# Issuing filler matmuls two at a time behind every second value step, in a fused attention and state-space kernel

## The chip, the cores and the metric

The kernel runs on one core of one Trainium2 chip, as one launch. The metric is the time of the launch on the device in microseconds, as the median of several runs; one more execution is taken with the hardware profiler, and its trace is what this document reads. Engines are called as the profile calls them: PE (TensorE's matmuls), PEld (its weight loads), DVE (VectorE), ACT (ScalarE), POOL (GpSimd) and SP (SyncE, which only issues DMAs here).

## The reference

Two independent results of 2048 x 640 are put side by side. The first is an attention in which each position sees only 8 earlier positions, 2 apart; the second is a long convolution (a state-space layer) done by Fourier transforms:

```python
# A: 32 heads of 20, window W = 8, dilation 2
q, k, v = split(x @ wqkv)                       # x: 2048 x 640
logits[h, s, w] = q[h, s] . k[h, s - 2 w] * 20 ** -0.5   # -1e9 where s - 2 w < 0
attn = softmax(logits, over w)
o[h, s] = sum_w attn[h, s, w] * v[h, s - 2 w]
a = o.reshape(2048, 640) @ wo
# B: K is a kernel of length L = 2048 for each of 640 channels, from 192 modes
K = Re sum_n Cc[d, n] * exp(dt[d] * A[d, n] * l) * dt[d] * Bc[d, n]
y = irfft(rfft(u padded to 2 L) * rfft(K padded to 2 L))[:L] + u * Dskip
out = concatenate([a, y], axis=-1)              # bf16, 2048 x 1280
```

## The kernel before

The kernel first makes the convolution's kernel K for five chunks of channels, transforms K and u, multiplies, and runs the first half of the inverse transform, whose result goes to DRAM (`Zd`). The attention's projections and logits are woven into the end of this. All that the change concerns is the last stage, from about 355 us on: the loop at the end of `body` (lines 847 to 888), where three kinds of work meet.

*Value steps.* The attention's sum over w is done by `Attention.av_step` (L608). The loop runs over 6 groups of (positions, head rows) and in each over w = 0 to 7, which makes 48 steps; the text numbers them s = 8·group + w. A step is one VectorE product of v with the weights (L618, into one of 6 ring buffers `ring`, so that product s + 6 can only be written when TensorE has read product s) and 16 matmuls of 32x32 tiles with the identity, which add the product up in two PSUM tiles `ps_o`. At w = 7 ScalarE copies the two tiles to `o` (L629); the tiles come from a pool of three, so the second half of the next group's first step waits for the first of these copies.

*Parts of the last inverse step.* `Inverse.part` (L676) makes 2 or 3 of the 64 rows l0 of y: 8 or 12 matmuls from a quarter of Z, which is loaded back from `Zd` by `Inverse.load` (L666) on SP's queue and, for the first and last quarter, also on POOL's; then one ScalarE copy to `ysb` (L687), and after each third part four writes of y on SP's queue (L690). There are 24 parts, p0 to p23, the last quarter of Z being read by p18 to p23. The ring of `ysb` has four places of three parts each.

*Output pieces.* `Attention.out_piece` (L631) makes a tile of 128 positions x 320 columns of `o @ wo`: 5 matmuls, one copy to `ob` (ScalarE, L645; VectorE, L643, for every second of the last eight), and after each second piece one write on POOL's queue (on SP's for the last four). Eight pieces come free with `out_proj` after each of the groups 1, 2, 4 and 5; they wait in the list `rest`, the parts in the list `parts`.

`fill(some, n)` (L839) issues the next n entries of a list. The parts and the pieces take their PSUM tiles from the same pool of two banks (`Attention.one`), in which the sums of the second softmax, `ps_s` (L572, matmuls at steps 6, 8, 11 and 14), hold one bank until `reciprocal` (L577) has read it, in VectorE's order after step 19.

`att.in_order()` (L833) makes TensorE's matmuls and ScalarE's copies of this stage keep the order in which the program issues them; VectorE's products keep it too. TensorE, ScalarE, VectorE and each DMA queue work their instructions off in order, so a wait of one instruction holds up all that stands behind it on its engine.

In group 1 one part follows each step from w = 2 on; in group 2 one piece each of the first three steps, five pieces the fourth, and one part each of the others; in groups 3 and 4 pieces and parts take turns, one behind each step; in group 5 one piece follows each step. What is left, the eight pieces of the last group, follows the loop.

Of the kernel before, what the change touches and what calls it, by code (L numbers as in the profile page):

```python
# [695 lines left out]
def body(tc, ctx, pools, prm, B_u, B_Dskip, Sd, Zd, UDd, A_x, A_wqkv, A_wo, out_a, out_b):  # L696
# [14 lines left out]
    with tc.tile_pool(name="prep_l", bufs=1) as pl, tc.tile_pool(name="prep_d", bufs=1) as pd, tc.tile_pool(name="prep_g", bufs=1) as pg, tc.tile_pool(name="prep_h", bufs=1) as ph, tc.tile_pool(name="psum_p", bufs=2, space=bass.MemoryType.PSUM) as psp:  # L711
        pools.update(prep_l=pl, prep_d=pd, prep_h=ph)
        pg.tile([128, GAP], bf16, name="gap")
        B, fill = partB_prep(tc, dict(pools, psum=psp), prm)
# [121 lines left out]
    parts = inv.parts()  # L836
    rest = []

    def fill(some, n=1):  # L839
        for f in some[0:n]:  # L840
            f()
        del some[0:n]
# [4 lines left out]
    for group, (i0, ni, j0, nj, done) in enumerate(GROUPS):  # L847
        for w in range(W):
            if group == 0:
                fill(parts, (0, 2, 0, 2, 0, 1, 0, 1)[w])  # L850
                if w == 3:
                    att.exp(1)
                if w in (0, 3):
                    att.proj_v(16 + 2 * (w == 3))
                if w == 5:
                    att.v_halo(8, 12)
            att.av_step(i0, ni, j0, nj, w)
            if 8 * group + w in LOADS:
                qr, c = LOADS[8 * group + w]
                inv.load(qr, c, c + 1)  # L860
            if 8 * group + w in (6, 8, 11, 14):
                n = (6, 8, 11, 14).index(8 * group + w)
                att.sums(2 * n, 2 * n + 2)
            if group == 0:
                if w == 2:
                    att.softmax_a(1)
                elif w == 7:
                    att.open_wo()
            elif group == 1:
                if w > 1:  # L870
                    fill(parts)
            elif group == 2:
                if w < 3:
                    fill(rest)
                elif w == 3:
                    att.reciprocal()
                    att.softmax_b(1)
                    fill(rest, 5)
                else:
                    fill(parts)  # L880
            elif group < 5:
                fill((rest, parts)[w % 2])
            else:
                fill(rest)
        if done is not None:
            rest += att.out_proj(done, done == 3)
    for f in parts + rest:
# [4 lines left out]
def kernel(  # L892
# [28 lines left out]
    Zd = dpool.tile([NCH, 128, 4096], bf16, name="Zdram")  # L921
    UDd = dpool.tile([NCH, 128, 2048], bf16, name="UDdram")
    body(tc, ctx, pools, prm, B_u, B_Dskip, Sd, Zd, UDd, A_x, A_wqkv, A_wo, out_a, out_b)


# [28 lines left out]
```

## Time and profile before

| | before |
|---|---|
| median of 3 runs | 432.25 us (431.16 to 433.85) |
| profiled execution, its own time | 431.36 us |
| its span, first to last instruction | 429.6 us |
| granted TensorE clock, mean | 0.925 |
| busy in the span | PE 361.9, DVE 379.9, ACT 313.0, POOL 39.4 us |
| TensorE instructions (matmuls) | 8693 |
| last stage: first value step's matmuls on TensorE | 360.44 us |
| first part that reads the last quarter of Z (p18) | 399.92 us |
| last value step's matmuls | 418.00 us |
| last copy of an output piece starts | 426.15 us |

The profile gives each instruction's start and duration, and for idle time in front of an instruction what ended it; "<-PE ps_o" means that a matmul writing `ps_o` released it, "<-issue" that nothing in the profile did. Matmuls are pipelined, so a row's duration overlaps the next row's: what a block of matmuls costs in a full queue is read from start to start. Helper functions give most matmuls and copies of this stage the line L429 or L430, so they are told apart by their tiles: `ps_o` for value steps, `ps_ib` for parts, `ps_op` for output pieces, `ps_s` for the sums.

### The profile page before, as it was taken

To read this page: it belongs to the slowest core of one execution; us is meant where nothing else is said; L and a number is where in the kernel's file an instruction comes from. 1 tells how busy PE (TensorE), PEld (TensorE's weight loads), DVE (VectorE), ACT (ScalarE), POOL (GpSimd) and SP (SyncE) were. 2 spreads that over 40 slices of the span, in tenths; PEclk is the share of its full clock that TensorE was granted. 3 is DMA by queue.
4 is the path that set the end of the run, shared out by engine and by line. 5 is a ranking of instruction groups with operands and counts; after the bars stand their busy time and mean duration, and the time that the engine had idled before them with its cause. 6 is when DMAs were issued, how large, how long until landed. Compare 5 with 4: busy or idle time off the path is not lost.

```text
span 429.6 us, 18968 instructions
## 1 busy us (share of the span) xinstructions
PE 361.9 (84%) x8693; PEld 266.2 (62%) x8693; DVE 379.9 (88%) x353; ACT 313.0 (73%) x574; POOL 39.4 (9%) x83
## 2 busy tenths in 40 slices
PE   1295779979997989879997799999799899889896
PEld 0184668867975778667875677545545666444443
DVE  8899997998997999999996989856978999999751
ACT  2984989789999989979997775333858446546543
POOL 7430000000000000000010000100000300501120
PEclk9999658999979898989996699999999999989999
DMA  5579203073233402424189842500030744988432
GB/s 146 169 168 191 31 3 125 29 243 82 99 125 127 99 30 101 161 90 101 40 305 211 195 101 104 215 2 3 13 88 2 207 78 148 241 207 238 112 96 92
DMA packets 45280, 51.76 MB, mean 120 GB/s; under 512 B 31392, under 2 KB 39136, under 8 KB 42512
## 3 DMA queue, kind: packets, MB, share of 16 engines
q1 hardware_dynamic: 41664, 41.47, 35.6%
q0 software_dynamic: 3392, 8.95, 7.1%
q8 instruction: 68, 1.11, 1.1%
q10 hardware_dynamic: 144, 0.12, 0.1%
q14 instruction: 12, 0.10, 0.1%
HBM read 28.08 MB, written 18.35 MB: 108 GB/s over the span
## 4 chain that ended last, share of the span: by engine, by line
PE 51%; ACT 20%; DVE 10%; issue 8%; SPq 5%; DMA 4%; POOL 2%; DVEq 0%; ACTq 0%; POOLq 0%
PE ps_k L325 8%; PE ps_k L330 7%; ACT A L345 7%; PE ps_ph L258 6%; PE ps_f L352 5%; PE ps_op L429 5%; PE ps_k L480 5%; SPq L674 3%; ACT R L232 3%; PE ps_q L498 3%; PE ps_ph L262 3%; DVE prod L531 2%; ACT Z L384 2%; ACT Sg L353 2%; PE ps_o L429 2%
## 5 line engine op out<-in xcount | busy, mean ns | idle before, releaser
L312 DVE TENSOR_TENSOR Y<-PG 128x3072 bf16<-128x3072 bf16 x60 | 103.2, 1751 | 7.4 <-PE ps_k L330 7.4
L258 PE MATMUL ps_ph<-LPC 128*64 128x256 bf16 x400 | 47.7, 340 | 13.6 <-DMA LPC<-lo 8.6
L325 PE MATMUL ps_k<-Y,X 128*32 128x64 bf16 x1920 | 47.3, 239 | 10.2 <-issue 6.3
L330 PE MATMUL ps_k<-Y,X 64*32 64x64 bf16 x1920 | 44.5, 234 | 3.5 <-issue 3.5
L325 PEld LDWEIGHTS <-X 128*32 128x32 bf16 x1920 | 32.4, 118 | 20.1 <-issue 12.2
L353 ACT CAST Sg<-ps_f 128x1024 bf16<-128x1024 f32 x40 | 37.7, 1039 | 7.4 <-PE ps_f L352 7.4
L232 ACT ACTIVATE R<-LPC 128x192 bf16<-128x192 f32 x155 | 41.8, 387 | 0.0
L345 ACT CAST A<-ps_f 128x1024 bf16<-128x1024 f32 x40 | 37.8, 1038 | 1.4 <-PE ps_f L344 1.4
L352 PE MATMUL ps_f<-A,T 128*64 128x128 bf16 x640 | 28.6, 265 | 11.8 <-ACT A L345 10.7
L330 PEld LDWEIGHTS <-X 64*32 64x32 bf16 x1920 | 30.0, 113 | 12.8 <-issue 5.2
L282 DVE TENSOR_TENSOR X<-R,TX 128x1536 bf16<-128x1536 bf16 x40 | 37.2, 951 | 0.0
L258 PEld LDWEIGHTS <-LPC 128*64 128x64 bf16 x400 | 23.7, 131 | 19.1 <-DMA LPC<-hi 8.6
L266 ACT ACTIVATE TX<-ps_ph 128x768 bf16<-128x768 int16 x40 | 30.4, 827 | 6.9 <-DVE X L282 4.3
L352 PEld LDWEIGHTS <-T 128*64 128x64 bf16 x640 | 26.9, 141 | 13.2 <-issue 12.9
L618 DVE TENSOR_TENSOR prod<-v,atp 128x2048 bf16<-128x2048 bf16 (+2 forms) x32 | 30.8, 1019 | 1.8 <-PE ps_o L429 1.8
L266 ACT ACTIVATE TA<-ps_ph 128x768 bf16<-128x768 int16 x40 | 30.3, 814 | 2.7 <-PE ps_ph L262 2.5
L262 PE MATMUL ps_ph<-LPC 128*64 128x128 bf16 x400 | 31.4, 255 | 0.0
L429 PE MATMUL ps_op<-wo,o 128*128 128x320 bf16 x160 | 27.2, 310 | 0.7 <-ACT ob L430 0.4
L262 PEld LDWEIGHTS <-LPC 128*64 128x64 bf16 x400 | 27.0, 136 | 1.2
L367 DVE TENSOR_TENSOR P<-P,Sg 128x4096 bf16<-128x4096 bf16 x10 | 22.9, 2286 | 2.4 <-DMA P<-Sdram 1.7
L430 ACT CAST ob<-ps_op 128x320 bf16<-128x320 f32 x28 | 11.9, 428 | 17.0 <-PE ps_op L429 15.1
L531 DVE TENSOR_TENSOR prod<-qT,kT 128x1024 bf16<-128x1024 bf16 (+1 forms) x16 | 23.0, 1482 | 0.5 <-ACT qT L499 0.5
(132 smaller groups left out, 677.4 us busy)
## 6 DMA issues: line engine op xcount, KB each, us to landing
Sdram<-Sg SPq DMA_DIRECT2D x5, 1024.0 KB
P<-Sdram SPq DMA_DIRECT2D x5, 1024.0 KB
P<-Sdram SPq DMA_DIRECT2D x10, 512.0 KB
Zdram<-Z SPq DMA_DIRECT2D x5, 1024.0 KB
Z<-Zdram SPq DMA_DIRECT2D x30, 128.0 KB
U<-in_B_u_dram SPq DMA_DIRECT2D x4, 640.0 KB
UDdram<-UD SPq DMA_DIRECT2D x10, 256.0 KB
out_dram<-ysb SPq DMA_DIRECT2D x32, 80.0 KB
```

The lines of the kernel that those rows point to most:

```text
L232: nc.scalar.activation(out=RX[:, :, e - 16, :], in_=src, func=ACT.Exp, scale=m)
L258: MM(o[64 * hh:64 * hh + 64, :, 0:8], lhsT=L[:, 64 * hh:64 * hh + 64], rhs=rhs, start=first, stop=last, skip_group_check=True, tile_positi ...
L262: MM(o[64 * hh:64 * hh + 64, :, 8:12], lhsT=L[:, 128:192], rhs=rhs[:, :, 16 * hh:16 * hh + 16], start=False, stop=last, skip_group_check=T ...
L266: last = nc.scalar.activation(out=dst, in_=words.rearrange("p b (q e f) -> p b q (e f)", e=8, f=4), func=ACT.Sin, scale=PI_LO / 32768.0)
L282: TT = lambda o, a, b, op: V.tensor_tensor(out=o, in0=a, in1=b, op=op)
L312: nc.vector.tensor_tensor(out=Y[:].rearrange("p q (b a) f -> p q b a f", a=8), in0=fa, in1=gb, op=A.mult)
L325: MM(ps[32 * g:32 * g + 32, t], lhsT=X[:, q, k, :, f], rhs=Ys[k][:, q, :, f], start=(t == 0 and k == 0), stop=False, tile_position=(0, 32 ...
L330: MM(ps[32 * g:32 * g + 32, t], lhsT=X[hb, q, k, :, f], rhs=Ys[k][hb, q, :, f], start=False, stop=(k == 2), tile_position=(64 * (g // 2), ...
L345: nc.scalar.copy(out=A1[:, :, 32 * b:32 * b + 32].rearrange("p k (j g) -> p k j g", g=4), in_=ps[:].rearrange("p j k g -> p k j g"))
L352: last = MM(ps[sl, kk], lhsT=C["T2"][:, 8 * b + kk, sl], rhs=A1[:, 8 * b + kk, :], start=(kk % 4 == 0), stop=True, skip_group_check=True, ...
L353: nc.scalar.copy(out=Sg[:, :, 8 * b:8 * b + 8, :], in_=ps[:].rearrange("p k (j g) -> p j k g", g=4))
L429: self.MM = lambda *a, **k: self.tc.keep_in_program_order(self.nc.tensor.matmul(*a, **k))
```

## The change

In groups 1 to 5 the fillers are issued behind every second step only, and two at once. Each list is worked off in its old order, and after each odd step as many fillers have been issued as before (in group 2 from w = 3 on), but with the kinds grouped otherwise: in groups 3 and 4 two pieces behind w = 1 and 5 and two parts behind w = 3 and 7, where pieces followed the even and parts the odd steps. In group 2 the three pieces of w = 0 to 2 come together behind w = 1. Group 0 and the work after the loop are the same.

```diff
             elif group == 1:
-                if w > 1:
-                    fill(parts)
+                if w in (3, 5, 7):
+                    fill(parts, 2)
             elif group == 2:
-                if w < 3:
-                    fill(rest)
+                if w == 1:
+                    fill(rest, 3)
                 elif w == 3:
                     att.reciprocal()
                     att.softmax_b(1)
                     fill(rest, 5)
-                else:
-                    fill(parts)
+                elif w in (5, 7):
+                    fill(parts, 2)
             elif group < 5:
-                fill((rest, parts)[w % 2])
-            else:
-                fill(rest)
+                if w % 2 == 1:
+                    fill((rest, parts)[w // 2 % 2], 2)
+            elif w % 2 == 1:
+                fill(rest, 2)
```

## The prediction

> **What bounds the kernel now.** The change touches only the last stage, so I read that stage: first busy time in short windows, then the order of time. Steps are numbered s = 8·group + w (0 to 47), the 24 parts of the inverse p0 to p23, the output pieces r (of 32). In the windows (columns: stretch, length, then busy us of PE, PEld, DVE, ACT, POOL, granted clock, DMA share, GB/s):
>
> ```profile
> 379.00:381.00 2.00, 0.76 (x24) 0.34 (x23) 2.00 (x2) 1.78 (x4) 0.00 (x0) 1.00 0.93 209
> 383.00:385.00 2.00, 2.00 (x23) 0.81 (x22) 2.00 (x3) 0.42 (x1) 0.55 (x1) 0.50 0.48 138
> 397.00:399.00 2.00, 1.41 (x37) 0.55 (x21) 2.00 (x4) 0.85 (x2) 0.54 (x1) 1.00 0.76 207
> 399.00:401.00 2.00, 1.08 (x31) 0.67 (x32) 0.43 (x2) 0.56 (x1) 0.00 (x0) 1.00 0.78 172
> 415.00:417.00 2.00, 2.00 (x42) 1.00 (x42) 0.00 (x0) 0.56 (x2) 0.54 (x1) 1.00 0.27 99
> ```
>
> Up to about 381 us VectorE is full and TensorE has holes. From there TensorE is behind: VectorE has ended step 47's product at 414.17 while TensorE reaches that step at 418.00. So TensorE's queue sets the end, with one thing from outside: a hole at 398 to 400. The order of time shows it, and what a block costs (start, duration, engine, line, operation, tile, count, idle before):
>
> ```profile
> 361.21 0.60 PE L429 MATMUL ps_ib<-Z,HB 96*32 96x160 bf16 x24 [0.33 <-DMA Z<-UDdram]
> 361.74 0.43 PE L429 MATMUL ps_o<-atp,ident 32*32 32x512 bf16 x16
> 361.96 0.42 PE L429 MATMUL ps_o<-prod,ident 32*32 32x512 bf16 x16
> ...
> 376.52 0.39 PE L429 MATMUL ps_ib<-Z,HB 96*32 96x160 bf16 x12 [0.21 <-ACT ysb L430]
> ...
> 379.31 1.75 DVE L577 RECIPROCAL tree<-ps_s 128x256 f32<-128x256 f32 x1
> ...
> 387.43 0.43 ACT L430 CAST ob<-ps_op 128x320 bf16<-128x320 f32 x1 [0.25 <-PE ps_op L429]
> 388.11 0.42 ACT L430 CAST ob<-ps_op 128x320 bf16<-128x320 f32 x1 [0.25 <-PE ps_op L429]
> ...
> 389.85 0.39 PE L429 MATMUL ps_ib<-Z,HB 96*32 96x160 bf16 x12
> 390.17 0.38 PE L429 MATMUL ps_o<-prod,ident 32*32 32x384 bf16 x16
> ```
>
> ```profile
> 399.92 0.39 PE L429 MATMUL ps_ib<-Z,HB 96*32 96x160 bf16 x12 [1.50 <-DMA out_dram<-ysb]
> ...
> 402.93 0.30 PE L429 MATMUL ps_o<-prod,ident 32*32 32x256 bf16 x8 [0.56 <-ACT o L430]
> ...
> 411.10 0.43 PE L429 MATMUL ps_o<-prod,ident 32*32 32x512 bf16 x16
> ...
> 411.47 0.85 PE L429 MATMUL ps_op<-wo,o 128*128 128x320 bf16 x5
> ...
> 412.25 0.43 PE L429 MATMUL ps_o<-atp,ident 32*32 32x512 bf16 x16
> ...
> 418.48 1.93 ACT L430 CAST o<-ps_o 128x1024 bf16<-128x1024 f32 x2
> 419.55 0.85 PE L429 MATMUL ps_op<-wo,o 128*128 128x320 bf16 x5 [0.33 <-ACT o L430]
> 420.79 5.27 PE L429 MATMUL ps_op<-wo,o 128*128 128x320 bf16 x35 [0.39 <-ACT ob L430]
> ```
>
> The block at 399.92 is p18, the first part that reads the last quarter of Z. The last loads of that quarter go out on SP's queue at 393.35 to 394.58; I take the hole as their landing, about 5.3 us later, though the row names a y write of the same queue.
>
> **The change part by part.** No matmul, copy, DMA or VectorE operation is added or removed. In the built program the orders of VectorE, POOL's queue and SP's queue stay as they were; only the order on TensorE and ScalarE differs.
>
> *Joined blocks.* A block pays for the change to another kind of block. A value step of 32x512 takes 0.37 ahead of a piece (411.10 to 411.47) but 0.22 ahead of another step (361.74 to 361.96): 0.15 saved. A piece takes 0.78 alone (411.47 to 412.25) and 0.68 in a row (ScalarE's copies at 387.43 and 388.11): 0.1. A part of 12 matmuls takes 0.32 alone (389.85 to 390.17), two joined 0.53 (361.21 to 361.74): 0.11. So two steps with two fillers save 0.26. From step 32 on there are 8 such pairs: 8 x 0.26 = **2.1 us saved**.
>
> [...]
>
> *Before p18.* p6 to p11 have one PSUM bank: the sums ps_s hold the other from step 6 to the reciprocal (379.31 + 1.75 = 381.06). Back to back, the second of a pair waits for the first one's copy: 0.12 + 0.56 + 0.04, some 0.7 for p7 and p9 each, with nothing between to cover it. p11 is worse: in the changed program it is the one that waits on VectorE, that is on the bank of ps_s, so it starts at 381.1 (before: 379.27, with a stall inside until 380.49, which then lies under the wait). Behind it in the queue stand steps 16 and 17 and the first pieces; VectorE's product 22 needs step 16's slot of the ring of 6, at 385, so nothing upstream is late. Walking the queue on with the block costs, half clock at 382.2 to 385.6 as in the profile, joins, and bank waits (0.4 before p15, 0.7 before the first piece after step 25, both because ScalarE's two copies of o stand ahead of the parts' copies), step 31 ends at 398.8.
>
> *p18.* It now stands behind steps 30 and 31 and one piece that followed it. SP's loads are not moved: the y writes ahead of them in SP's queue wait for p8 and p11, whose copies end at 376.7 and 382.0 while SP comes to them at 385.49 and 388.88. So p18 still starts at 399.9, after a wait of 1.0 now, and p19 ends at 399.9 + 0.53 = 400.4, where the kernel before has the same work done at 402.07: **1.66 saved**. All that was lost or won ahead of 398.8 is swallowed here; if TensorE comes later than 399.9 each us counts.
>
> *Waits removed and added from step 32 on.* Removed, start to start less the block's own cost: step 32 (402.07 to 403.17 less 0.26 = 0.84, o copy), p20 0.10, step 40 (409.36 to 410.32 less 0.37 = 0.59), the first and second last-row pieces (419.55 - 418.37 - 0.79 = 0.39; 420.79 - 419.55 - 0.74 = 0.50): 2.4. Added: the first piece after step 33 waits for p18's copy, which stands behind the o copies (1.93): 0.67; likewise after step 41 0.63, step 40 0.2, p21 and p23 0.1; and at the end two pieces instead of one follow step 47, their copies behind the o copies, so the first last-row piece waits for its bank: 0.1 + 1.93 + 0.42 + 0.04 after step 47, less two pieces (1.36) = 1.13. Sum 2.7. Net **0.3 lost**. Bounds: all of the added waits gone, 2.7 better; every one of the 8 pairs waiting 0.65, 5.2 instead of 2.7, 2.5 worse. I take 2.7, because each is a copy queue worked out from rows.
>
> Sum: -2.1 - 1.66 + 0.3 = **-3.5 us**. VectorE gets step 47's product out at 412.5, 1 us ahead of TensorE, so it does not take over. The last copy ends at 423.2 instead of 426.64, the tail of 3 us (last write) stays: span 426.1, the profiled execution 431.36 - 3.5 = 427.9. That execution lies 0.9 below the median shown, so against the median 432.25: **428.8 us**.
>
> **Rivals.** *Clock (the slower one).* The half clock at 382.2 to 385.6 follows a stretch with PE 0.76 busy of 2.00; elsewhere holes of like size (397 to 401) cost none. The change puts longer idle into places: 2 us before p11, 1.0 at p18, 0.6 twice, 1.1 at the end. Each further half-clock stretch of 3.4 us, length as in the profile, costs up to 1.7 where TensorE sets the end. It decides from the third such stretch after 385.6 on: 428.8 + 5.1 = 433.9, slower than before. Against it: 399 to 401 with 1.08 busy of 2.00 was followed by full clock. One or two stretches: 430.5 to 432.2. [...]
>
> *Bank waits at every pair.* If both banks of a pair are still being copied each time: 2.5 worse, 431.3. Against: in groups 4 and 5 two steps (0.37 to 0.58) and the sister block lie between a filler and its bank's next use.
>
> *More gained.* If Z's last loads land by 398.8 (1.0 more) and half of the added waits do not come (1.35): 426.4. For it: the landing is one execution's.
>
> *No effect of the change itself* is ruled out by the built order of TensorE.
>
> **How the numbers follow.** Forecast (427.3 to 430.2) 0.55; more gained 0.16; one or two half-clock stretches 0.15; bank waits 0.08; three stretches or a mishap of that size 0.06. Range 426.2 to 432.8: it leaves out the far ends of the first and last. A change of 1% (4.3 us, below 427.9 or above 436.6) is about what a measurement of this kernel tells from none. Faster by more: all but little of "more gained" and a fifth of the forecast, 0.28; slower by more: needs five stretches, 0.06; else 0.66.
>
> **What would show it.** Right: p11 right behind the reciprocal; p18 at about 400 with an idle of 1 us or less ahead; joined steps of 32 matmuls at 0.58 and pieces of ten at 1.47; step 47 ended near 414, last-row pieces from 416.5. Wrong: the last quarter of Z landing elsewhere than near 400, half clock behind 386, or steps waiting on VectorE's products in groups 4 and 5.

## The result, and the profile after

| | before | after | again (the changed kernel, a second run) |
|---|---|---|---|
| median | 433.05 us (20 runs, 428.38 to 440.55) | 427.98 us (20 runs, 426.22 to 431.72) | 429.04 us (7 runs) |
| ratio to before, 95% interval | | 0.9922 [0.9897, 0.9947] | 0.9892 [0.9847, 0.9937] |
| profiled execution, its own time | 431.36 us | 426.76 us | 425.3 us |
| its span | 429.6 us | 425.0 us | 423.5 us |
| first value step | 360.44 | 358.62 | 358.54 |
| p18 starts | 399.92 | 398.16 | 397.46 |
| p18 behind the first value step | 39.48 | 39.54 | 38.92 |
| step 47 starts | 418.00 | 412.75 | 411.29 |
| last copy starts | 426.15 | 421.57 | 420.11 |
| from p18 to the last copy | 26.24 | 23.41 | 22.65 |
| from the first value step to the last copy | 65.71 | 62.95 | 61.57 |

The changed kernel is 0.8% faster (some 3.4 us), 1.1% in the second comparison. The prediction said 428.8 us and a gain of 3.5 us. The ratio leaves out executions more than 1.5% above the fastest of their kernel, so it lies nearer to 1 than the quotient of the two medians, which are over all executions.

Single executions scatter by over 1%, so two spans must not simply be subtracted. Of the 4.6 us between the profiled spans, 1.8 us lie ahead of the first value step (360.44 against 358.62), where both kernels issue the same. The table's last two rows leave this out. From p18 on, TensorE sets the end, and this stretch fell by 2.83 us, and by 3.59 us in the second run. The rest of this document is read by it, with one reservation: it counts the work that now stands ahead of p18 (two steps and a piece) as saved, which is right only where p18 waits for Z in both orders. The last row, over the whole stage, does not depend on that; it fell by 2.76 and 4.14 us.

The order of time of the changed kernel around its old stalls (start, duration, engine, line, operation, tile, count, idle before):

```profile
377.48 1.76 DVE L577 RECIPROCAL tree<-ps_s 128x256 f32<-128x256 f32 x1
379.29 0.32 PE L429 MATMUL ps_ib<-Z,HB 96*32 96x160 bf16 x8 [1.50 <-DVE tree L577]
...
395.25 1.93 ACT L430 CAST o<-ps_o 128x1024 bf16<-128x1024 f32 x2 [0.16 <-PE ps_o L429]
398.16 0.96 PE L429 MATMUL ps_ib<-Z,HB 96*32 96x160 bf16 x24 [2.96 <-DMA out_dram<-ysb]
399.05 0.65 PE L429 MATMUL ps_o<-prod,ident 32*32 32x256 bf16 x32
...
408.43 0.65 PE L429 MATMUL ps_o<-atp,ident 32*32 32x512 bf16 x32
409.02 1.53 PE L429 MATMUL ps_op<-wo,o 128*128 128x320 bf16 x10
410.48 0.65 PE L429 MATMUL ps_o<-prod,ident 32*32 32x512 bf16 x32
...
413.22 1.93 ACT L430 CAST o<-ps_o 128x1024 bf16<-128x1024 f32 x2
...
415.53 5.95 PE L429 MATMUL ps_op<-wo,o 128*128 128x320 bf16 x40 [0.89 <-ACT ob L430]
421.57 0.49 DVE L643 CAST ob<-ps_op 128x320 bf16<-128x320 f32 x1 [0.98 <-PE ps_op L429]
```

Four things are to be seen. p11 (379.29) stands right behind the reciprocal. p18 and p19 are now one block of 24 matmuls behind one wait, which is longer than before (2.96 instead of 1.50). Two steps cost 409.02 - 408.43 = 0.59, two pieces 410.48 - 409.02 = 1.46. And a new wait of 0.89 stands ahead of the last row's pieces, for a copy of `ob` that follows the o copies on ScalarE.

The windows around p18 (stretch, length, busy us of PE, PEld, DVE, ACT, POOL, granted clock, DMA share, GB/s):

```profile
395.00:397.00 2.00, 0.20 (x16) 0.00 (x0) 2.00 (x4) 1.84 (x3) 0.54 (x1) 1.00 0.91 244
397.00:399.00 2.00, 0.84 (x24) 0.67 (x24) 0.74 (x2) 0.37 (x2) 0.00 (x0) 0.81 0.86 219
399.00:401.00 2.00, 2.00 (x42) 0.97 (x39) 1.29 (x2) 0.83 (x2) 0.00 (x0) 0.50 0.39 82
401.00:403.00 2.00, 2.00 (x58) 1.05 (x56) 0.49 (x1) 1.04 (x3) 0.05 (x1) 0.83 0.17 39
```

The hole is followed by half clock (0.50), from 398.2 to 401.7, in steps on which the end now depends. The second run of the same kernel has a smaller hole, no half clock behind it, and the smaller of the two stretches to the end:

```profile
397.46 0.60 PE L429 MATMUL ps_ib<-Z,HB 96*32 96x160 bf16 x24 [1.31 <-DMA out_dram<-ysb]
397.99 0.44 PE L429 MATMUL ps_o<-prod,ident 32*32 32x256 bf16 x32
398.63 1.52 PE L429 MATMUL ps_op<-wo,o 128*128 128x320 bf16 x10 [0.21 <-ACT ysb L430]
...
405.53 1.52 PE L429 MATMUL ps_op<-wo,o 128*128 128x320 bf16 x10 [0.33 <-ACT ysb L430]
...
414.07 5.95 PE L429 MATMUL ps_op<-wo,o 128*128 128x320 bf16 x40 [0.89 <-ACT ob L430]
```

### The profile page after: what moved, and what is told of

Read it like the earlier page. It is cut to its first block, busy times and chain, and to the rows that moved or that the text cites. A ratio compares the mean times of both kernels' runs of the same rounds, so it can differ in the third digit from the quotient of the medians.

```text
span 425.0 us, 18968 instructions
## 1 busy us (share of the span) xinstructions
PE 351.9 (83%) x8693; PEld 261.5 (62%) x8693; DVE 379.0 (89%) x353; ACT 312.0 (73%) x574; POOL 39.1 (9%) x83
## 5 line engine op out<-in xcount | busy, mean ns | idle before, releaser
L258 PE MATMUL ps_ph<-LPC 128*64 128x256 bf16 x400 | 43.7, 317 | 16.0 <-DMA LPC<-lo 8.7
L258 PEld LDWEIGHTS <-LPC 128*64 128x64 bf16 x400 | 21.7, 122 | 21.7 <-issue 16.9
L262 PE MATMUL ps_ph<-LPC 128*64 128x128 bf16 x400 | 29.0, 240 | 0.0
L429 PE MATMUL ps_op<-wo,o 128*128 128x320 bf16 x160 | 24.9, 307 | 1.6 <-ACT ob L430 0.9
L262 PEld LDWEIGHTS <-LPC 128*64 128x64 bf16 x400 | 24.5, 126 | 0.8
L282 DVE TENSOR_TENSOR PG<-R,TA 128x3072 bf16<-128x3072 bf16 x10 | 17.5, 1752 | 6.5 <-ACT TA L266 6.5
```

What stands on the lines that cost most here:

```text
L258: MM(o[64 * hh:64 * hh + 64, :, 0:8], lhsT=L[:, 64 * hh:64 * hh + 64], rhs=rhs, start=first, stop=last, skip_group_check=True, tile_positi ...
L262: MM(o[64 * hh:64 * hh + 64, :, 8:12], lhsT=L[:, 128:192], rhs=rhs[:, :, 16 * hh:16 * hh + 16], start=False, stop=last, skip_group_check=T ...
L282: TT = lambda o, a, b, op: V.tensor_tensor(out=o, in0=a, in1=b, op=op)
```

## The experiments

The theories, by the letters that the expectations use. A: the prediction's account (p18 covered, cheaper joins from step 32 on, small bank waits). B: the gain is the luck of where the half clock fell. C: joined blocks pay wherever they stand. D: p11's wait for the reciprocal costs something at the end. E: the pairs of groups 1 and 2 move a half-clock stretch from ahead of p18, where the wait for Z hides it, to behind it, where it costs. F: with two PSUM banks, longer runs of one kind wait. G: the o copy sets the end.

### The changed kernel again

No edit; what can differ is the execution.

> The changed kernel once more, as the yardstick of this batch. A (the prediction's account: blocks joined from step 32 on, p18 covered by steps 30 and 31): 3.5 us below the kernel before; from p18's start to the last VectorE copy of a piece about 23 us in the trace (before: 26.2). B (the gain is luck of the half clock): the trace shows no half clock behind 386 us or p18 at another place, and the gain goes with it.

Measured: 0.9892 [0.9847, 0.9937]. From p18 to the last copy 22.65 without half clock behind p18, against 23.41 with a stretch of 3.4 us. The second run holds a break of some 0.5 us besides (below), so the stretch cost about 0.8 + 0.5 = 1.3 us, less than the forecast's 1.7 (an estimate: half of the 3.4 at a granted clock of 0.50). In the kernel before, a piece and a step that took 1.08 from start to start at full clock (381.11 to 382.19) took 1.91 at half clock (382.19 to 384.10). The gain is there with and without it, so B is out as the cause.

### The change in three parts

Groups 1 and 2 alone, the rest as before:

```diff
             elif group == 1:
-                if w > 1:
-                    fill(parts)
+                if w in (3, 5, 7):
+                    fill(parts, 2)
             elif group == 2:
-                if w < 3:
-                    fill(rest)
+                if w == 1:
+                    fill(rest, 3)
...
-                else:
-                    fill(parts)
+                elif w in (5, 7):
+                    fill(parts, 2)
```

> Groups 1 and 2 in pairs, groups 3 to 5 as before. A: 0.0 us against the kernel before, since p18 still starts when the last quarter of Z has landed; the wait ahead of p18 may be longer or shorter than 1.5 us, p18's start to the last copy stays 26.2 us. C (joins pay wherever they are): 6 joins of steps and 5 of fillers, about 1.4 us faster. D (the wait of p11 for the reciprocal costs time at the end): 0.5 to 1 us slower.

Group 3 alone:

```diff
-            elif group < 5:
+            elif group == 3:
+                if w % 2 == 1:
+                    fill((rest, parts)[w // 2 % 2], 2)
+            elif group == 4:
                 fill((rest, parts)[w % 2])
```

> Group 3 in pairs, the other groups as before. A: p18 starts at the landing as before, but with steps 30 and 31 and a piece done, so p19 ends 1.7 us earlier behind it; 1.7 to 2.2 us faster in all. C: 4 pairs at 0.26, 1.0 us. B: nothing steady.

Groups 4 and 5 alone:

```diff
+            elif group == 3:
+                fill((rest, parts)[w % 2])
             elif group < 5:
-                fill((rest, parts)[w % 2])
-            else:
-                fill(rest)
+                if w % 2 == 1:
+                    fill((rest, parts)[w // 2 % 2], 2)
+            elif w % 2 == 1:
+                fill(rest, 2)
```

> Groups 4 and 5 in pairs, groups 1 to 3 as before. A: p18's wait and place as in the kernel before, 8 joins of 0.26 less 0.3 to 0.7 of bank waits: 1.4 to 1.8 us faster, all of it behind p19. C: 2.1 us. B: nothing steady.

And groups 3 to 5 together, the change without its first two hunks:

> Groups 3, 4 and 5 in pairs, groups 1 and 2 one by one as in the kernel before. A: nothing ahead of p18 counts, so the same 3.5 us as the whole change. E (pairs in groups 1 and 2 only move the half clock from the stretch ahead of p18, where the wait for Z hides it, to the stretch behind, where it costs 1.7 us): up to 1.9 us better than the whole change, about 5 us below the kernel before; half clock in the trace ahead of p18, none behind.

| | ratio to before, 95% interval | last matmul's start to p18 | half clock behind p18 | p18 to last copy |
|---|---|---|---|---|
| groups 1, 2 | 1.0043 [1.0007, 1.0079] | 3.42 | 404.7 to 411.5 | 28.49 |
| group 3 | 0.9968 [0.994, 0.9996] | 0.63 | 402.1 to 408.9 | 27.72 |
| groups 4, 5 | 0.9951 [0.9915, 0.9988] | 0.70 | none | 24.66 |
| groups 3 to 5 | 0.992 [0.9888, 0.9952] | 2.75 | 403.1 to 406.5 | 23.34 |

(Third column: from the start of the last matmul ahead of p18 to the start of p18; in the kernel before 1.89, after 3.33, again 1.69.) All of the gain is in groups 3 to 5: 0.992 like the whole change, and the two halves add up to it (-0.32% and -0.49%). Groups 4 and 5 gain 26.24 - 24.66 = 1.58 us from p18 on. For group 3 the profile alone would mislead, since its execution had 6.8 us of half clock behind p18; as an estimate, less what two stretches cost at 1.3 to 1.7 us each, it is 24.3 to 25.1, a gain of 1.1 to 1.9. C is refuted: the pairs of groups 1 and 2 save the same changes from one kind of block to another and bring nothing. E had forecast for groups 3 to 5 alone no half clock behind p18 and up to 1.9 us more than the whole change; neither came. The order of time of groups 1 and 2 alone shows where it goes:

```profile
400.25 0.43 PE L429 MATMUL ps_o<-prod,ident 32*32 32x512 bf16 x16
403.72 0.39 PE L429 MATMUL ps_ib<-Z,HB 96*32 96x160 bf16 x12 [3.03 <-DMA out_dram<-ysb]
```

TensorE is there sooner and stands longer: p18 starts 39.39 us behind the first value step, before 39.48. What is saved ahead of p18 is waited for at p18. Then the clock, in the windows of the same kernel:

```profile
402.00:404.00 2.00, 0.28 (x12) 0.22 (x12) 0.24 (x1) 0.00 (x0) 0.00 (x0) 1.00 0.93 221
404.00:406.00 2.00, 2.00 (x45) 0.79 (x37) 0.69 (x1) 0.83 (x2) 0.00 (x0) 0.67 0.61 138
...
408.00:410.00 2.00, 2.00 (x45) 0.78 (x43) 0.83 (x2) 1.14 (x3) 0.00 (x0) 0.50 0.00 0
```

The same kernel was run once more, to see whether the loss and this picture belong together:

> Groups 1 and 2 alone in pairs, once more. A: no difference from the kernel before, the +0.4% of the first time chance. E (half clock moved behind p18, where it costs): again 0.3 to 0.5% slower, and in the trace an idle of about 3 us ahead of p18 with half clock right behind it.

Measured: 0.9992 [0.9959, 1.0025]; the profile had the same picture (3.0 ahead of p18, half clock 402.6 to 409.4, 28.44 to the last copy). The picture came twice, the loss once. That groups 1 and 2 cost time, through D or E, is therefore not shown; a gain was seen in neither comparison, and the first excludes the 1.4 us of C.

### The part that reads the last quarter of Z, without its wait

In the kernel before and in the changed one, p18 to p23 read the third quarter, which has long been there; all loads stay. The parts then make other numbers of the same size.

```diff
-... rhs=self.t[qr][:, g, :, l + i, :] ...
+... rhs=self.t[min(qr, 2)][:, g, :, l + i, :] ...
```

> The kernel before, with p18 to p23 reading the third quarter of Z where they should read the last, so that p18 waits for no load; all loads and writes go out as before, and the last quarter of y is another number. A: p18 right behind step 29, 1.6 to 2.0 us faster than the kernel before. If the wait were not on the path: 0.

```profile
397.98 0.43 PE L429 MATMUL ps_o<-prod,ident 32*32 32x512 bf16 x16
398.34 0.39 PE L429 MATMUL ps_ib<-Z,HB 96*32 96x160 bf16 x12
398.67 0.43 PE L429 MATMUL ps_o<-atp,ident 32*32 32x512 bf16 x16
```

Measured: 0.9966 [0.9934, 0.9998], some 1.5 us. In the order of time p18 follows step 29 without idle; it starts 37.93 us behind the first value step instead of 39.48, and from p18 to the last copy there are 26.23 us as before. So the hole at p18 was waiting for Z, though the row names a y write, and all of it was on the path in this pair of executions: 1.55 us. The packet records of the traces say the same of both kernels: the loads of Z are the 1024-byte packets of SP's queue, and the last of them ends at 398.67 before, at 396.83 after and at 396.38 in the second run, 1.1 to 1.3 us ahead of p18 each time.

> The changed kernel with the same exchange: p18 reads the third quarter of Z and waits for no load. A: the copies of o behind step 31 (1.93 us) and those of p18 and p19 then set when the next pieces get their banks, so only what the wait was beyond 1 us comes back: 0.5 to 2.3 us below the changed kernel, 4 to 6 below the kernel before. E: no idle of 3 us ahead of p18, and no half clock behind it.

```profile
399.22 0.60 PE L429 MATMUL ps_ib<-Z,HB 96*32 96x160 bf16 x24
399.34 1.93 ACT L430 CAST o<-ps_o 128x1024 bf16<-128x1024 f32 x2 [0.16 <-PE ps_o L429]
400.40 0.41 PE L429 MATMUL ps_o<-prod,ident 32*32 32x256 bf16 x24 [0.35 <-ACT o L430]
401.15 1.04 ACT L430 CAST ysb<-ps_ib 128x480 bf16<-128x480 f32 x2
401.78 0.43 PE L429 MATMUL ps_op<-wo,o 128*128 128x320 bf16 x2 [0.97 <-ACT ysb L430]
```

Measured: 0.9887 [0.9849, 0.9925], beside 0.9922 and 0.9892 of the changed kernel with its wait; the intervals overlap, so of the 0.5 to 2.3 us that A forecast nothing is shown. p18 comes 1.4 us sooner (37.54 behind the first value step, against 38.92), but the o copies start no sooner than step 31's end, and behind them come step 32's second half (0.35) and the copies of p18 and p19, which the next piece waits for (0.97). With the wait for Z, this ScalarE time lay under it. So in the changed kernel other waits stand where the wait for Z was: taking it away gives nothing that these comparisons can tell from none.

### Longer runs

Groups 4 and 5 with four fillers behind every fourth step:

```diff
-            elif group < 5:
+            elif group == 3:
                 if w % 2 == 1:
                     fill((rest, parts)[w // 2 % 2], 2)
-            elif w % 2 == 1:
-                fill(rest, 2)
+            elif group == 4:
+                if w % 4 == 3:
+                    fill((rest, parts)[w // 4], 4)
+            elif w % 4 == 3:
+                fill(rest, 4)
```

> The changed kernel with groups 4 and 5 in fours: four pieces or four parts behind w = 3 and w = 7. A: 4 more joins of two steps (0.15) and 4 of fillers (0.11), 1.0 us saved, less 0.5 for banks (the third and fourth part of a run wait for copies of 0.56; four pieces in a row do not wait): 0.5 us faster than the changed kernel. F (two banks make any run longer than two wait): pieces wait too, 1 to 2 us slower than the changed kernel.

```profile
410.48 0.79 PE L429 MATMUL ps_ib<-Z,HB 96*32 96x160 bf16 x20 [0.97 <-ACT ysb L430]
...
412.27 2.94 PE L429 MATMUL ps_op<-wo,o 128*128 128x320 bf16 x20
...
415.14 1.13 PE L429 MATMUL ps_o<-prod,ident 32*32 32x512 bf16 x64
416.21 1.53 PE L429 MATMUL ps_op<-wo,o 128*128 128x320 bf16 x10
416.27 1.93 ACT L430 CAST o<-ps_o 128x1024 bf16<-128x1024 f32 x2 [0.54 <-PE ps_o L429]
418.58 2.65 PE L429 MATMUL ps_op<-wo,o 128*128 128x320 bf16 x18 [0.84 <-ACT ob L430]
```

Measured: 0.9926 [0.9889, 0.9962], as with pairs; from p18 to the last copy 22.88, against 22.65. Steps 32 to 47 take 12.12 instead of 13.30 (again), and step 47 to the last copy 10.22 instead of 8.82. The two must be taken together, because four pieces instead of two stand behind step 47, so that some 1.5 us of work has passed from the first stretch to the second. Together they are 22.35 against 22.12, or against 21.6 without the break of the second run. F holds only for the parts: the third part of a run waits (0.97), but four pieces run without idle between them (412.27), as A said. The waits for copies from p18 to the end are 0.57, 0.97 and 0.84, together 2.38, against 1.43 with pairs; these grew by 0.95 and the whole by 0.76, so by difference, as an estimate, the further joins saved some 0.2, where A forecast 1.0.

### The wait at the end

In the changed kernel, the last two pieces ahead of the last row are copied by VectorE, which has ended its products by then, instead of by ScalarE behind the o copies (the same flag puts their write on SP's queue instead of POOL's):

```diff
-... self.out_piece(q, sc, eh, last and eh == 1)) ...
+... self.out_piece(q, sc, eh, last and eh == 1 or q == 2 and sc == 3)) ...
```

> The changed kernel, with the copies of the last two pieces ahead of the last row (those behind step 47) on VectorE, which is idle by then, and their write on SP's queue. A (the first last-row piece waits 1.1 us because those copies stand behind the two copies of o on ScalarE): the wait of 0.9 to 1.1 us is gone, last step to last copy about 7.7 us instead of 8.8, the kernel 1.0 us faster than the changed one, 4.5 below the kernel before. G (the copy of o itself sets the end): no gain.

```profile
413.83 0.65 PE L429 MATMUL ps_o<-prod,ident 32*32 32x512 bf16 x32
414.41 7.45 PE L429 MATMUL ps_op<-wo,o 128*128 128x320 bf16 x50
414.52 1.93 ACT L430 CAST o<-ps_o 128x1024 bf16<-128x1024 f32 x2
415.36 0.49 DVE L643 CAST ob<-ps_op 128x320 bf16<-128x320 f32 x1 [2.25 <-ACT ob L430]
...
421.95 0.49 DVE L643 CAST ob<-ps_op 128x320 bf16<-128x320 f32 x1 [0.98 <-PE ps_op L429]
```

Measured: 0.9873 [0.9848, 0.9899], 427.5 us, the fastest measured beside the next. All 50 matmuls of the last ten pieces are one row without idle, and step 47 to the last copy takes 7.90 instead of 8.82: the 0.89 wait was on the path, and with the same two banks it goes when the copies leave ScalarE's order. G is out: the o copies stand where they stood (414.52).

The same without the pairs of groups 1 and 2:

> The same two copies on VectorE, and pairs in groups 3 to 5 only. A: like the kernel with pairs everywhere and these copies, 4.5 us below the kernel before, since nothing ahead of p18 counts.

Measured: 0.9853 [0.9814, 0.9892], 427.64 us, within the other's interval: once more groups 1 and 2 make no difference. Both versions beat the kernel before; against the changed kernel (0.9922 and 0.9892) they were compared through the kernel before only, and there the intervals overlap, so that they beat it too rests on the 0.92 us in the trace.

### The kernel before again

> The kernel before once more, for its trace. E: half clock of 3.4 us or more between 378 and 390, ahead of p18, an idle of 2 us or less at p18, no half clock behind it; p18 to the last copy 26.2 us.

Measured: 1.0001 [0.996, 1.0041]. Its half clock lay elsewhere (381.0 to 384.4 and 394.6 to 398.0), its p18 came 40.65 us behind the first value step, and from there to the last copy it took 26.23 us. The second stretch made TensorE late, and the idle ahead of p18 was 0.23 instead of 1.50: how much of a wait there is to fill differs from execution to execution. So with TensorE at full clock behind p18 this stretch is 26.2 in three profiles of the old order (26.24, 26.23, and 26.23 with the other quarter of Z) and 22.65 in the one such profile of the changed kernel.

## Why the prediction was right, point by point

**The sum.** Forecast -3.5 us; measured -0.78% of 433.05, or 3.4 us, and in the two profiles where no half clock follows p18, 26.24 - 22.65 = 3.59. By the forecast's own terms these 3.59 are 2.0 from joined blocks (forecast 2.1), 1.62 from p18 and p19 (1.66), 2.4 from waits removed (2.4), less 1.9 for waits added (2.7) and less a break of 0.5 that no term named; the joins are what is left when the rest is taken off. So the two large terms came true one by one, but that the whole came within 0.1 is in part luck: the break took back most of what the smaller waits had given.

**Joined blocks.** Right in size. From step 42 to 44 and from 44 to 46 the old order takes 2.30 each in all three of its profiles, the new one 2.04 to 2.05 in all seven profiles with it: 0.25 to 0.26 a pair, as forecast. Why a change from one kind of block to another costs this was not shown.

**p18 and p19.** Right in the number, in part by luck. p18 started 39.54 and 38.92 us behind the first value step (39.48 before), with steps 30 and 31 and a piece ahead of it, and what the old order did until 402.07 cost 2.15 from p18 on and now 0.53 (397.46 to 397.99): 1.62 against a forecast of 1.66. But two details were wrong and came out even. SP's loads were said not to move: the last one was issued 35.61 and 35.18 us behind the first value step, against 34.14 before (35.22 in the other profile of the kernel before, so most of this lies in the scatter). And Z was said to land 5.3 us after that issue: p18 followed it by 3.93 and 3.74. The packets show that this is the load itself, whose last packet ends 4.1 us behind the issue before and 2.6 and 2.7 in the changed kernel. Why it lands sooner was not found; that both end near 39 us could be one cause or chance.

**The size of the wait at p18.** Wrong: forecast 1.0, measured 2.96 and 1.31. The failed step is the walk to "step 31 ends at 398.8", 38.4 us behind the first value step, which took half clock at 382.2 to 385.6 over from the profile before. Neither run of the changed kernel had it there: the first eight pieces took 385.37 - 380.02 = 5.35 from first to last, before 388.59 - 381.11 = 7.48, and step 31 ended at 36.6 and 37.6 instead. The second run was the later one because it had half clock elsewhere ahead of p18 (375.4 to 378.8), and so its hole was the shorter one. Nothing of this was gained, as the step itself said of everything ahead of p18, but the clock rival came true in small behind the longer hole: one stretch in one of two runs, about 1.3 us.

**Bank waits.** Right in place, too large in size. Taken as the forecast took them, start to start less the block's own cost, they are in the second run: at the piece after step 33, 0.64 - 0.37 = 0.27 (forecast 0.67; idle alone 0.97 where Z's wait is taken away); at steps 40 and 41, 1.23 - 0.58 = 0.65 (0.2 and 0.63); at p21 and p23 together 0.06 (0.1); at the end 2.42 - 1.47 = 0.95 (1.13). Together that is 1.9 of 2.7. The second run lost some 0.5 of the difference again between steps 36 and 38, which took 2.37 there and 1.83 in the first: a break inside step 36 that the profile gives to nothing ("issue"):

```profile
401.04 0.28 PE L429 MATMUL ps_o<-atp,ident 32*32 32x256 bf16 x3
401.58 0.43 PE L429 MATMUL ps_o<-atp,ident 32*32 32x256 bf16 x29 [0.25 <-issue]
```

**The end.** The forecast had step 47 ended near 414 and the last copy's start near 422.7 (0.5 ahead of its end at 423.2), 8.7 us apart; in both runs it is 8.46 (413.11 to 421.57), the end's wait being smaller. The last row's pieces stood at 415.53, not at 416.5, since that execution reached this stage 1.8 us sooner.

**The rivals.** Bank waits at every pair: no, the second run has three rows of waits for a copy from p18 to the end. Three half-clock stretches behind 385.6: no; one, in one run of two. Half clock behind 386 was one of the prediction's signs of being wrong, and in that run it showed; the gain outweighed it. Whether bank waits bring half clock on, the traces do not settle. From p18 on, the bank waits of 0.2 to 0.9 us of the changed kernel were not followed by half clock; the hole of 3 us was. Ahead of p18, half clock set in at 375.4 in the second run, right behind three bank waits of p7 to p9:

```profile
373.42 0.39 PE L429 MATMUL ps_ib<-Z,HB 96*32 96x160 bf16 x12 [0.66 <-ACT ysb L430]
374.47 0.32 PE L429 MATMUL ps_ib<-Z,HB 96*32 96x160 bf16 x8 [0.18 <-ACT ysb L430]
375.31 0.53 PE L429 MATMUL ps_ib<-Z,HB 96*32 96x160 bf16 x12 [0.52 <-ACT ysb L430]
```

The changed order without Z's wait had the same (from 378.6); the first run had the same three waits and full clock behind them. In the second run the stretch was hidden by the wait for Z that came after it. More gained: not by the way described, but the experiment at the end got 0.9 us of the added waits back.

## What to carry to other kernels

Where an engine with a full queue meets one fixed arrival, put work that needs nothing ahead of the waiting block, and count only what is saved behind the arrival; savings ahead of it turned into a longer wait here (3.03 us instead of 1.50 with groups 1 and 2 alone). When blocks are joined to save changes from one kind to another, look at what stands next in the copying engine's queue: here a short copy behind two long ones set when a PSUM bank came free, and moving the two short copies to an idle engine gave 0.9 us in the trace, where joining further gave nothing that could be measured. Where single executions scatter by 1%, measure between two events of the same stage, not between two spans.

## What the runs showed of the hardware

**Half clock came in whole stretches of 3.4 us, and holes of 2.1 to 3.0 us were followed by one.** In the profiles of these runs every half-clock stretch between the first value step and the last copy was 3.4 or 6.8 us long. Of fourteen profiles, six had 2.48 us or more from the last matmul's start to p18, that is 2.11 to 3.03 us of idle (after 3.33, groups 1 and 2 alone 3.42 and 3.0, groups 3 to 5 2.75, the two with the tail's copies moved 2.48 and 2.65), and each was followed by half clock within 1 us of p18's start. Of the eight with 1.89 or less none was, but for group 3 alone, where half clock came 3 us later (402.1), behind two windows of moderate work and a bank wait of 1.08:

```profile
399.00:401.00 2.00, 1.13 (x40) 0.75 (x41) 2.00 (x4) 2.00 (x3) 0.54 (x1) 1.00 0.81 198
401.00:403.00 2.00, 1.62 (x45) 0.76 (x44) 0.53 (x2) 1.22 (x3) 0.00 (x0) 0.78 0.25 64
```

```profile
401.38 0.84 PE L429 MATMUL ps_op<-wo,o 128*128 128x320 bf16 x5 [1.08 <-ACT ysb L430]
```

The gap's length alone does not settle it: here half clock came behind a wait of 1.08, and in the second run of the changed kernel a wait of 1.31 ahead of p18 was followed by full clock (1.00 from 397 to 401). What does was not found.

**Half clock ahead of this stage differs from execution to execution.** Up to 355 us, where all these kernels issue the same instructions, the profiles have between 44.4 us (again) and 61.4 us (before) at half clock. It does not order the executions by itself: 47.8 us go with a first value step at 358.62 (after) and with one at 364.33 (groups 1 and 2 alone). What makes single executions scatter by 1% was not found.

**What was ready stood behind what its engine had ahead of it.** In the kernel before, the matmuls of the sums end at 378.28 (377.15 + 1.13), and the reciprocal starts at 379.31, as the VectorE products ahead of it end (377.57 + 1.82); the copy of p8 ended at 376.47, and its writes went out on SP's queue at 385.49, behind nine loads of Z (378.75 to 385.39). A wait held up what stood behind it, too: without the wait for Z, p18 and all that TensorE had behind it came 1.55 us sooner against the first value step, and the 0.89 us ahead of the last row's pieces went when two copies left ScalarE's order.
